# TensorE's small products of a chunked recurrence are queued group by group

## The chip, the cores and the metric

The kernel runs on one core of one Trainium2 chip. Times are device microseconds (us) of one execution. The core has five engines with a queue each, worked off in order: TensorE (PE, its weight loads PEld), VectorE (DVE), ScalarE (ACT), GpSimd (POOL) and SyncE (SP, which issues most DMAs). An instruction that waits for another engine holds up all that stands behind it in its queue.

## The reference

Three stages on [4 batches, 768 steps, 320 channels]. The first is a recurrence over the steps with a 40x40 state for each of 32 batch-heads; the second a feed-forward layer with a convolution of three steps and a gate; the third an attention with four experts of which two count.

```python
for t in range(S):                                   # state: [B, H, 40, 40]
    y[:, :, t] = einsum('bhd,bhde->bhe', r_t, state)
    Sa = einsum('bhde,bhe->bhd', state, a_t)
    state = state * w_t - einsum('bhd,bhe->bhde', Sa, b_t) + einsum('bhd,bhe->bhde', v_t, k_t)
x = relu-feed-forward(y): h = max(y @ w_in, 0); out = h * sigmoid(conv3(h)) @ w_out
out = attention of 4 experts on x, the best 2 of each row weighted by their gate
```

## The kernel before, in words

The recurrence is cut into chunks of 32 steps (24 chunks, `k`), two of which make a block of 64 (12 blocks, `n`). Three generators write its work. `prep(n)` forms for a block what doesn't depend on the state: decays on VectorE, the pairwise products of the inputs, and the inverse of a triangular matrix for each head. `chain(k)` carries the state over a chunk; each link needs the one before. `post(k)` forms the chunk's outputs. All three use TensorE for small products: 16 or 32 in a group (`mm`, L161), each on its own tiles of the PE array, or 4 transposes (`tr`, L165). In the trace and in the instruction order a group is known by what its products read:

- prep: `kb,a` (pairwise products, 32 products, two groups a block), `cst,kb` (transposes, four groups a block), `O,g` and `M,d` (inverse, 32 each, one group a block);
- chain: `SV,a` (32), `cst,sT` (transposes of the state, two groups), `X,T` (32), `VZ,KB` (16); ScalarE copies each result out before the next group can start (X at L360, VZ at L376, the new state SV in two instructions at L409), VectorE forms the new state (sT, L402 and L404);
- post: `cst,U` (transposes), `ra,VT` (16), `RB,LB` (32), with VectorE's mask RB (L441) and result xe (L455).

That makes 286 groups. A product in full float32 leaves two matmul records in the trace, a transpose one.

The feed-forward layer (`ff`, 128x128 matmuls at L561 and L584) runs beside the recurrence, and attention (L694 to L830) follows; the last part of the feed-forward layer runs beside the start of attention. `merge` calls the generators by due times: every `yield` tells when the next piece is due, `self.work` adds up what the small products are thought to cost, and the feed-forward layer advances by that sum.

What is called first has the higher priority. The order on every engine is then made by the tile framework when the program is built: it plays the program through on a timeline of its own, and gives each engine at each moment the ready instruction with the highest priority. So products of one group can be parted by products of another that became ready meanwhile and rank higher. [...]

Of the kernel before, what the change touches and what calls it, by code (L numbers as in the profile page):

```python
# [49 lines left out]
class Kernel:  # L50
# [103 lines left out]
    def load_rb(self, k):  # L154
        for h in range(2):
            self.nc.sync.dma_start(self.RB[R[1 - h], h].rearrange("p u a t -> p (u a t)"), self.i["rb"][k, 40 * h:40 * h + 40])

    def mm(self, ns, *a, **k):

        self.work += ns  # L160
        self.nc.tensor.matmul(*a, **k)  # L161

    def tr(self, ns, *a):
        self.work += ns
        self.nc.tensor.transpose(*a)  # L165

    def prep(self, n):
        nc, wk = self.nc, self.wk
        w, P, a, kb = self.w, self.P[n % 3], self.a[n % 2], self.kb
# [9 lines left out]
        for k in range(1, 5):  # L179
            x = early("xd", [128, 32, 16], "L1") if k == 1 else wk.tile([128, 32, 32 >> k], F32, name=f"L{k}", bufs=1)  # L180
# [34 lines left out]
        for u0 in (0, 8):  # L215
            us = slice(u0, u0 + 8)
            FG = self.ps[2][:, 0 if 0 < n < EN or n == 0 and u0 == 0 else 1].rearrange("p (u x s) -> p u x s", u=8, x=2)
            for u in range(8):
                for q in range(4):
                    be, r = q // 2, R[q % 2]  # L220
                    self.mm(WF, FG[32 * q:32 * q + 32, u].rearrange("p x s -> p (x s)"), a[r, be, q % 2, u0 + u],
                            kb[r, u0 + u, be].rearrange("p x s -> p (x s)"), start=True, stop=True)
                if u % 2:
                    yield 0.26 + 0.07 * (u0 > 0) + 0.015 * (u + 1) / 2
            nc.scalar.activation(Gp[:, us], FG[:, :, 1], AF.Copy)
            nc.vector.transpose(F[:, us], FG[:, :, 0])
            nc.gpsimd.tensor_tensor(F[:, us], F[:, us], self.mask[:, None].to_broadcast([128, 8, 32]), op=ALU.mult)
            yield 0.33 + 0.07 * (u0 > 0)
# [31 lines left out]
        def turn(u0):  # L260

            kp = self.ps[2][:, 1].rearrange("p (u x) -> p u x", u=4)
            for u in range(4):
                self.tr(WK, kp[:, u, :104], kb[E, u0 + u].rearrange("p b x t -> p (b x t)"), self.ident[:104, :104])
            nc.scalar.activation(KB[:, u0:u0 + 4], kp.rearrange("p u (h e) -> p u h e", h=2)[:, :, :, :40], AF.Copy)  # L265
# [16 lines left out]
        x = (8, 8)  # L282
# [25 lines left out]
        yield 0.72  # L308

        def blocks(out, lhs, rhs, x):  # L310
            for u in range(8):
                for q in range(0, 128, 32):
                    s = slice(q, q + 32)
                    self.mm(WS, out[s, u], lhs[s, u], rhs(s, u), start=True, stop=True)
                if u % 2:
                    yield x + 0.02 * (u + 1) / 2


        Mp = self.ps[2][:, 1, :256].rearrange("p (u x) -> p u x", u=8)
# [11 lines left out]
    def chain(self, k):  # L331
        nc, wk, t = self.nc, self.wk, self.t[k // NC]
        U, KB, u0 = self.U[k % 2], t["KB"], NP * (k % NC)
        zero = k == 0
        sT, sN = self.sT[k % 2], self.sT[(k + 1) % 2]

        def st(x):
            y = x[E]
            return bass.AP(tensor=y.tensor, offset=y.offset, ap=[list(y.ap[0]), [104, NP], [64, 2], [1, 40]])

        So, SV = self.S[k % 2], self.SV

        def back(p0):
            Sp = self.ps[3][:, 0].rearrange("p (m x) -> p m x", m=4)
            for p in range(4):
                self.tr(WR, Sp[E, p, :104], sT[E, p0 + p], self.ident[:104, :104])
            nc.scalar.activation(So[E, p0:p0 + 4], Sp[E].rearrange("p m (a e) -> p m a e", a=2)[:, :, :, :40], AF.Copy)

        cu = self.ps[0]
        Xp = cu[:, 0, :320].rearrange("p (m d) -> p m d", m=NP)  # L350
        for p in range(NP):
            for al in range(2):
                for be in range(2):
                    q = 32 * (2 * be + al)
                    r = slice(0, 96 + 8 * al)
                    self.mm(XA, Xp[q:q + 32, p], t["a"][r, be, al, u0 + p], SV[r, al, be, p], start=True, stop=True)
            if p == 3:
                yield 0.06
        X = wk.tile([128, NP, 40], F32, name="X", bufs=1)
        nc.scalar.activation(X, Xp, AF.Copy)  # L360
        yield 0.14
        if not zero:
            back(0)
            yield 0.25
        for p in range(NP):
            for al in range(2):
                for be in range(2):
                    q = 32 * (2 * be + al)
                    s, o = slice(q, q + 32), 64 * be + 32
                    self.mm(WX, cu[o:o + 32, al, p * 40:p * 40 + 40], t["T"][s, u0 + p], X[s, p], start=True, stop=True)  # L370
        VZ = self.VZ
        for be in range(2):
            s = slice(64 * be + 32, 64 * be + 64)
            y = VZ[s, :, :, be].rearrange("p m a d -> p a m d")
            z = cu[s, :, :320].rearrange("p a (m d) -> p a m d", m=NP)
            nc.scalar.activation(y, z, AF.Copy, scale=-1.0)  # L376
        yield 0.4
        if not zero:
            back(4)
            yield 0.5  # L380
        for p in range(NP):
            for al in range(2):
                self.mm(WD, cu[R[al], p // 4, 80 * (p % 4):80 * (p % 4) + 80], KB[:, u0 + p, al],
                        VZ[:, p, al].rearrange("p b d -> p (b d)"), start=True, stop=True)
        for be in range(2):
            s = slice(64 * be + 32, 64 * be + 64)
            for r in range(2):
                y, z = U[64 * r + 32 * be:64 * r + 32 * be + 32], VZ[s, r::2, :, be]
                y = bass.AP(tensor=y.tensor, offset=y.offset, ap=[list(y.ap[0]), [104, NP // 2], [64, 2], [1, 40]])
                if UD:  # L390
                    for al in range(2):
                        nc.sync.dma_start(U[64 * r + 32 * be:64 * r + 32 * be + 32, :, 64 * al:64 * al + 40], VZ[s, r::2, al, be])
                else:
                    nc.scalar.activation(y, z, AF.Copy)
        qq = t["q0"][E, u0:u0 + NP, :, None].to_broadcast([104, NP, 2, 40])
        for h in range(2):
            ps = slice(4 * h, 4 * h + 4)
            Dv = cu[E, h, :320].rearrange("p (m b d) -> p m b d", m=4, b=2)
            if zero:
                nc.vector.tensor_tensor(st(sN)[:, ps], Dv, qq[:, ps], op=ALU.mult)  # L400
            else:
                nc.vector.tensor_tensor(st(sN)[:, ps], Dv, st(sT)[:, ps], op=ALU.add)  # L402
        if not zero:
            nc.vector.tensor_tensor(st(sN), st(sN), qq, op=ALU.mult)  # L404
        if k + 1 < NT * NC:
            for al in range(2):
                y = sN[R[al]]
                y = bass.AP(tensor=y.tensor, offset=y.offset, ap=[list(y.ap[0]), [64, 2], [104, NP], [1, 40]])
                nc.gpsimd.tensor_copy(SV[R[al], al], y) if al < SC else nc.scalar.activation(SV[R[al], al], y, AF.Copy)  # L409
        if k + 1 < NT * NC:  # L410
            self.load_v(k + 1)
        yield 1.0

    def post(self, k):
# [10 lines left out]
        if c == 0:  # L425
            t["xe"] = wk.tile([128, NP, 2, TOK], F32, name="xe", bufs=1)
        vp = (self.ps[1] if k < BK else self.ps[3])[:, 0].rearrange("p (u x) -> p u x", u=4)
        for p in range(4):
            self.tr(WV, vp[E, p], self.U[k % 2][:, p], self.ident)
        nc.scalar.activation(VT[E].rearrange("p u b x -> p (u b) x")[:, :, 32:], vp[E].rearrange("p u (b t) -> p (u b) t", t=32), AF.Copy)  # L430
        yield 0.16
        ap = self.ps[3][:, 1].rearrange("p (u a t) -> p u a t", u=NP, a=2)
        for p in range(NP):
            for be in range(2):
                self.mm(WA, ap[64 * be:64 * be + 64, p], VT[E, p, be], ra[E, p, be], start=True, stop=True)
            if p == 3:
                yield 0.3
        for be in range(2):
            s = slice(64 * be, 64 * be + 64)
            y = RB[s, be].rearrange("p u a t -> p (u a) t")  # L440
# [2 lines left out]
        if k + 1 < NT * NC:  # L443
            self.load_ra(k + 1)
            self.load_vt(k + 1)
        yp = (self.ps[1] if k < BK else self.ps[3])[:, 1].rearrange("p (m b t) -> p m b t", m=NP, b=2)
        for p in range(NP):
            for be in range(2):
                r = slice(0, 104 + 24 * be)
                for al in range(2):  # L450
                    self.mm(WY, yp[R[al], p, be], LB[r, be, p, al], RB[r, be, p, al], start=True, stop=True)
            if p % 4 == 3:
                yield 0.55 + 0.05 * p
        pp = P.rearrange("p (c m b) t -> p c m b t", c=NC, b=2)[E, c]
        nc.vector.tensor_tensor(t["xe"][E, :, :, 32 * c:32 * c + 32], yp[E], pp, op=ALU.mult)  # L455
        yield 0.92
# [566 lines left out]
```

## Time and profile before

| | us |
|---|---|
| median of 3 runs | 898.44 (894.2 to 899.88) |
| the profiled execution's own time | 899.17 |
| its span, first to last instruction | 897.4 |
| recurrence with the feed-forward layer | about 45 to 590 of the span |
| attention alone | from about 650 on |

The profile is one execution, so sums are made against 899.17. Busy times of PE are modelled: matmuls overlap, so the time that a group takes is read from one start to the next, not from its length.

### The profile page before, as it was taken

The numbers are of one execution on the slowest core, as the hardware profiler recorded it, in microseconds if no ns is written. First come the engines' busy times: TensorE is split into PE (matmuls) and PEld (weight loads), VectorE is DVE, ScalarE is ACT, GpSimd is POOL, SyncE is SP. The second block draws the span as 40 slices with busy tenths as digits, with TensorE's granted clock in tenths as the row PEclk, the third lists the DMA queues.
The fourth block names the chain that finished last, engine by engine and source line by source line (L and its number), as shares of the span: only waits on it lengthen the run. The fifth ranks groups of instructions, "written<-read, shape, count | busy, mean of one in ns | idle before, by whom it ended". The sixth has DMA issues, their size and how long they took to land.

```text
span 897.4 us, 31509 instructions
## 1 busy us (share of the span) xinstructions
PE 748.3 (83%) x13112; PEld 657.7 (73%) x13112; DVE 693.9 (77%) x1541; ACT 574.4 (64%) x1355; POOL 377.6 (42%) x419
## 2 busy tenths in 40 slices
PE   1257768997988989888798879869999999999988
PEld 1146556785877977777687868859878888888876
DVE  5888896999898898787887984575677767876664
ACT  0156655866675767584758567758877666775565
POOL 6063545433335243322334242754644343443352
PEclk9999577997989799897979889979999999999999
DMA  5435673555564464545545534440011101110001
GB/s 129 94 122 125 166 167 86 134 127 127 116 158 104 99 152 108 132 99 130 129 113 120 117 86 93 90 127 16 15 46 37 46 16 31 37 38 16 23 8 38
DMA packets 143489, 81.17 MB, mean 90 GB/s; under 512 B 113859, under 2 KB 127043, under 8 KB 142387
## 3 DMA queue, kind: packets, MB, share of 16 engines
q1 hardware_dynamic: 138450, 74.34, 34.1%
q0 software_dynamic: 4896, 4.83, 2.5%
q8 instruction: 103, 1.69, 0.8%
q14 instruction: 40, 0.32, 0.1%
HBM read 51.63 MB, written 11.80 MB: 71 GB/s over the span
## 4 chain that ended last, share of the span: by engine, by line
PE 42%; DVE 24%; ACT 11%; DMA 10%; issue 7%; POOL 4%; SPq 1%; ACTq 0%; DVEq 0%; POOLq 0%
PE ps L161 8%; PE ps L561 5%; PE ps L584 5%; PE ps L815 4%; DVE cv L596 4%; PE ps L712 4%; PE ps L798 4%; PE ps L165 3%; PE ps L703 2%; PE ps L762 2%; PE ps L830 2%; DMA kb<-in_kb_e_dram 2%; DVE kb L205 2%; PE ps L763 2%; DVE Q L198 2%
## 5 line engine op out<-in xcount | busy, mean ns | idle before, releaser
L784 POOL TENSOR_TENSOR A<-A,rs 128x128 f32<-128x128 f32 (+5 forms) x96 | 87.7, 935 | 113.7 <-DVE rs L782 95.6
L596 DVE SCALAR_TENSOR_TENSOR cv<-h,cw,cv 128x256 f32<-128x256 f32 (+1 forms) x192 | 97.1, 550 | 38.5 <-ACT cv L594 37.7
L599 POOL TENSOR_TENSOR cv<-cv,h 128x512 f32<-128x512 f32 (+1 forms) x48 | 61.4, 1280 | 133.2 <-ACT cv L598 123.6
L561 PE MATMUL ps<-xl,win 128*128 128x256 f32 x384 | 97.1, 304 | 4.5 <-POOL xl L539 3.6
L561 PE MATMUL ps<-xh,win 128*128 128x256 f32 x384 | 96.5, 309 | 4.9 <-ACT xh L537 4.3
L584 PE MATMUL ps<-wout,gh 128*128 128x320 f32 x384 | 90.4, 330 | 2.6 <-ACT gh L478 2.5
L479 POOL TENSOR_TENSOR gl<-cv,gh 128x512 fp32r<-128x512 f32 x48 | 62.5, 1303 | 53.5 <-ACT gh L478 46.9
L769 ACT ACTIVATE A<-ps,nm 128x128 f32<-128x128 f32 (+5 forms) x96 | 60.7, 633 | 37.0 <-DVE nm L767 28.9
L561 PEld LDWEIGHTS ps<-xh,win 128*128 128x128 f32 x384 | 73.2, 210 | 7.0 <-ACT xh L537 4.6
L561 PEld LDWEIGHTS ps<-xl,win 128*128 128x128 f32 x384 | 73.1, 208 | 6.0 <-POOL xl L539 4.1
L767 DVE TENSOR_REDUCE nm<-ps 128x1 f32<-128x128 f32 (+5 forms) x96 | 58.8, 619 | 20.5 <-PE ps L765 8.9
L584 PEld LDWEIGHTS ps<-wout,gh 128*128 128x128 f32 x384 | 66.0, 200 | 4.9 <-ACT gh L478 4.1
L161 PE MATMUL ps<-kb,a 40*32 40x64 f32 x1536 | 34.3, 239 | 34.7 <-DVE kb L205 31.1
L584 PE MATMUL ps<-wout,gl 128*128 128x320 f32 x192 | 59.0, 330 | 0.3 <-issue 0.3
L165 PE MATMUL ps<-cst,kb 104*128 104x104 f32 x192 | 33.3, 307 | 29.4 <-ACT KB L265 16.4
L161 PE MATMUL ps<-RB,LB 104*40 104x32 f32 (+1 forms) x1536 | 47.9, 215 | 11.1 <-DMA RB<-in_rb_dram 5.0
L161 PEld LDWEIGHTS ps<-kb,a 40*32 40x32 f32 x1536 | 28.1, 120 | 39.0 <-issue 19.1
L161 PEld LDWEIGHTS ps<-RB,LB 104*40 104x40 f32 (+1 forms) x1536 | 41.6, 131 | 17.3 <-DVE cv L596 4.6
L798 PE MATMUL ps<-cid,A 128*128 128x128 f32 x336 | 52.9, 276 | 1.5 <-ACT AT L803 0.7
L762 PE MATMUL ps<-k,q 128*128 128x256 f32 (+3 forms) x144 | 49.3, 351 | 5.3 <-ACT A L769 3.8
L712 PE MATMUL ps<-x,wqk 128*128 128x384 f32 x256 | 53.2, 347 | 0.3 <-ACT yt L622 0.3
L598 ACT ACTIVATE cv<-cv 128x512 f32<-128x512 f32 (+1 forms) x48 | 30.3, 630 | 30.7 <-DVE cv L596 30.4
(177 smaller groups left out, 2191.6 us busy)
## 6 DMA issues: line engine op xcount, KB each, us to landing
kb<-in_kb_e_dram SPq DMA_DIRECT2D x24, 320.0 KB
LB<-KB SPq DMA_DIRECT2D x48, 160.0 KB
LB<-S SPq DMA_DIRECT2D x46, 100.0 KB
a<-in_a_e_dram SPq DMA_DIRECT2D x24, 160.0 KB
VT<-in_vt_dram SPq DMA_DIRECT2D x48, 80.0 KB
RB<-in_rb_dram SPq DMA_DIRECT2D x48, 80.0 KB
SV<-in_v_dram SPq DMA_DIRECT2D x48, 80.0 KB
VZ<-in_v_dram SPq DMA_DIRECT2D x96, 40.0 KB
```

The lines of the kernel that those rows point to most:

```text
L161: self.nc.tensor.matmul(*a, **k)
L165: self.nc.tensor.transpose(*a)
L479: (eng or self.nc.vector).tensor_tensor(lo, x, hi.bitcast(F32), op=ALU.subtract)
L561: nc.tensor.matmul(hp[:, dd], wt[:, 128 * d:128 * d + 128], x, start=k == 0, stop=k == 7)
L584: nc.tensor.matmul(self.ps[1][:, tb, :DM], x, wt, start=d == 0 and k == 0, stop=d == 7 and k == 2)
L596: nc.vector.scalar_tensor_tensor(y, h[:, dd, :, k:k + nt], self.cw[:, k, d:d + 1], y, op0=ALU.mult, op1=ALU.add)
L599: (nc.gpsimd if GM and st % GM == 0 and st >= GN else nc.vector).tensor_tensor(cv[:, :, :, :nt], cv[:, :, :, :nt], h[:, :, :, 1:1 + nt], o ...
L712: nc.tensor.matmul(pp, self.wqk[:, wk, hl, 128 * m:128 * m + 128], x[:, xk], start=j == 0, stop=j == 7)
L762: nc.tensor.matmul(sp[:, c0:c1], q[:, ce, 128 * j:128 * j + 128], k[:, ce, c0:c1], start=True, stop=False)
L769: nc.scalar.activation(A[:, :nk], sp[:, :nk], AF.Exp, bias=nm, accum_out=sums[:, e:e + 1])
L784: nc.gpsimd.tensor_tensor(A[:, :nk], A[:, :nk], rs[:, e:e + 1].to_broadcast([128, nk]), op=ALU.mult)
L798: nc.tensor.transpose(tp[:, m, e], As[e][:, 128 * (2 * g + m):128 * (2 * g + m) + 128], self.cid)
```

## The change

A group begins with `burst()`, which clears `head`. The group's first product is then issued at its own priority and kept as `head`. Every later one goes through `follow`: it is put behind `head` in PE's queue (`issue_after`), and ranks 3000 places higher, ahead of all that is ready. The due times inside a group are dropped: `yield` stands once, after the group. No product is added, removed or altered, and no tile or buffer either. Lines up to 157 keep their numbers; after it they move by 10 to 14, L161 and L165 become L172 (heads) and L175 (the rest).

```diff
+    def burst(self):
+
+        self.head = None
+
     def mm(self, ns, *a, **k):
+        self.follow(ns, self.nc.tensor.matmul, *a, **k)
+
+    def tr(self, ns, *a):
+        self.follow(ns, self.nc.tensor.transpose, *a)
+
+    def follow(self, ns, f, *a, **k):
 
         self.work += ns
-        self.nc.tensor.matmul(*a, **k)
-
-    def tr(self, ns, *a):
-        self.work += ns
-        self.nc.tensor.transpose(*a)
+        if self.head is None:
+            self.head = f(*a, **k).ins
+            return
+        with self.tc.issue_after(self.head), self.tc.high_priority(offset=3000):
+            f(*a, **k)
...
+            self.burst()
             for u in range(8):
                 for q in range(4):
                     be, r = q // 2, R[q % 2]
                     self.mm(WF, FG[32 * q:32 * q + 32, u].rearrange("p x s -> p (x s)"), a[r, be, q % 2, u0 + u],
                             kb[r, u0 + u, be].rearrange("p x s -> p (x s)"), start=True, stop=True)
-                if u % 2:
-                    yield 0.26 + 0.07 * (u0 > 0) + 0.015 * (u + 1) / 2
+            yield 0.26 + 0.07 * (u0 > 0) + 0.06
...
+        self.burst()
         for p in range(NP):
             for be in range(2):
                 r = slice(0, 104 + 24 * be)
                 for al in range(2):
                     self.mm(WY, yp[R[al], p, be], LB[r, be, p, al], RB[r, be, p, al], start=True, stop=True)
-            if p % 4 == 3:
-                yield 0.55 + 0.05 * p
+        yield 0.8
```

The other groups get `self.burst()` in the same way. More due times go or move: in `blocks` four become one, in `chain` that of SV,a moves to the group's end, in `post` that inside ra,VT is dropped.

Two places of PE's queue show it. A row is a line of the kernel, the operation, out<-in and the size, with a count where it repeats; a number behind a name is that of its buffer. The first place is in chunk 21: PE's queue before, with post's group RB,LB of chunk 20 in three pieces, the chain's SV,a and X,T of chunk 21 in two each, and prep's transposes (cst,kb) inside X,T.

```order
L161 MATMUL ps<-SV,a_81 32x40 x23
L161 MATMUL ps<-kb,a_82 32x64 x32
L161 MATMUL ps<-SV,a_81 32x40 x9
L165 MATMUL ps<-cst,sT_96 104x104 x4
L161 MATMUL ps<-RB,LB_85 40x32 x22
L161 MATMUL ps<-X,T 32x40 x10
L165 MATMUL ps<-cst,kb 128x104 x4
L161 MATMUL ps<-X,T 32x40 x22
L161 MATMUL ps<-RB,LB_85 40x32 x9
L165 MATMUL ps<-cst,kb 128x104 x4
L161 MATMUL ps<-RB,LB_85 40x32
```

The same RB,LB and X,T in PE's queue of the changed kernel, with what stands behind them.

```order
L172 MATMUL ps<-RB,LB_85 40x32
L175 MATMUL ps<-RB,LB_85 40x32 x31
L172 MATMUL ps<-cst,kb 128x104
L175 MATMUL ps<-cst,kb 128x104 x3
L172 MATMUL ps<-X,T 32x40
L175 MATMUL ps<-X,T 32x40 x31
L575 MATMUL ps<-xl,win 128x256 x2
L598 MATMUL ps<-wout,gh 128x320 x4
L172 MATMUL ps<-cst,kb 128x104
L175 MATMUL ps<-cst,kb 128x104 x3
```

Both groups stand whole; one set of prep's transposes is now ahead of X,T, the other behind it and behind feed-forward matmuls.

The second place is in chunk 11: PE's queue before, where the chain's VZ,KB cuts into post's RB,LB of chunk 10.

```order
L161 MATMUL ps<-RB,LB_85 40x32 x16
L161 MATMUL ps<-VZ,KB 40x80 x16
L161 MATMUL ps<-RB,LB_85 40x32 x15
L165 MATMUL ps<-cst,kb 128x104 x4
L161 MATMUL ps<-RB,LB_85 40x32
L165 MATMUL ps<-cst,U_92 104x128 x4
```

The same place in the changed kernel.

```order
L172 MATMUL ps<-RB,LB_85 40x32
L175 MATMUL ps<-RB,LB_85 40x32 x31
L172 MATMUL ps<-VZ,KB 40x80
L175 MATMUL ps<-VZ,KB 40x80 x15
L172 MATMUL ps<-cst,kb 128x104
L175 MATMUL ps<-cst,kb 128x104 x3
```

RB,LB is not cut any more, and the chain's VZ,KB stands behind all 32 of its products instead of behind 16.

## Rows read from the trace of the kernel before

**Rows 1.** The page: span, busy times, the chain by engine.

```profile
span 897.4 us, 31509 instructions
PE 748.3 (83%) x13112; PEld 657.7 (73%) x13112; DVE 693.9 (77%) x1541; ACT 574.4 (64%) x1355; POOL 377.6 (42%) x419
PE 42%; DVE 24%; ACT 11%; DMA 10%; issue 7%; POOL 4%; SPq 1%; ACTq 0%; DVEq 0%; POOLq 0%
```

**Rows 2.** Stretches: length, busy time of each engine, PE clock, DMA share, GB/s.

```profile
45.00:320.00 275.00, 221.38 (x5386) 193.15 (x5387) 237.73 (x459) 179.96 (x389) 118.90 (x122) 0.86 0.54 128
320.00:590.00 270.00, 228.93 (x5182) 206.77 (x5181) 214.18 (x404) 180.14 (x399) 106.90 (x108) 0.90 0.50 115
590.00:650.00 60.00, 53.95 (x370) 50.38 (x370) 38.75 (x91) 47.49 (x110) 32.31 (x36) 0.96 0.15 38
650.00:898.00 248.00, 234.89 (x1973) 199.95 (x1971) 170.66 (x509) 160.95 (x445) 103.30 (x124) 1.00 0.10 30
```

**Rows 3.** Chain by line, of 45 to 320 and of 320 to 590.

```profile
by line: PE ps L161 10.9%; issue 9.2%; PE ps L561 5.7%; DMA kb<-in_kb_e_dram 4.5%; DVE cv L596 4.5%; DVE kb L205 4.2%; PE ps L165 4.0%; PE ps L584 3.0%; DVE t L274 2.7%; ACT SV L409 2.6%; DMA xs<-xe 2.2%; DVE Q L198 2.1%; DMA xd<-xs 2.0%; A
...
by line: PE ps L161 15.6%; issue 10.3%; PE ps L584 7.8%; PE ps L561 7.5%; DVE cv L596 6.0%; DMA RB<-in_rb_dram 4.3%; PE ps L165 4.2%; DMA xs<-xe 3.1%; DMA LB<-S 2.3%; DVE Q L198 2.1%; DVE kb L205 2.1%; DMA SV<-in_v_dram 1.9%; DVE a L209 1.6
```

**Rows 4.** Stretches: PE and PEld busy with L161 alone, then with L165 alone.

```profile
45.00:320.00 275.00, 122.67 (x4736) 104.81 (x4736) 0.86 0.54 128
320.00:590.00 270.00, 100.40 (x4288) 86.62 (x4288) 0.90 0.50 115
...
45.00:320.00 275.00, 42.49 (x240) 28.36 (x240) 0.86 0.54 128
320.00:590.00 270.00, 32.89 (x216) 22.13 (x216) 0.90 0.50 115
```

**Rows 5.** Timeline of PE from 302.5: start, length, instruction, records; chunk 11's place.

```profile
302.55 0.81 PE L161 MATMUL ps<-RB,LB 104*40 104x32 f32 x32
303.18 1.29 PE L161 MATMUL ps<-VZ,KB 128*40 128x80 f32 x32
304.30 0.77 PE L161 MATMUL ps<-RB,LB 104*40 104x32 f32 x30
305.00 0.58 PE L165 MATMUL ps<-cst,kb 104*128 104x104 f32 x4
305.50 0.26 PE L161 MATMUL ps<-RB,LB 128*40 128x32 f32 x2
305.69 0.65 PE L165 MATMUL ps<-cst,U 128*104 128x128 f32 x4
```

**Rows 6.** Timeline of PE from 545.7: whole groups X,T, RB,LB and VZ,KB.

```profile
545.77 0.79 PE L161 MATMUL ps<-X,T 32*32 32x40 f32 x64
546.49 1.42 PE L161 MATMUL ps<-RB,LB 104*40 104x32 f32 x64
547.83 0.56 PE L584 MATMUL ps<-wout,gh 128*128 128x320 f32 x2
...
550.99 1.31 PE L161 MATMUL ps<-VZ,KB 128*40 128x80 f32 x32
552.22 0.53 PE L165 MATMUL ps<-cst,U 128*104 128x128 f32 x3
```

**Rows 7.** Timeline of PE from 518.9: chunk 21's place, [idle before <-releaser].

```profile
518.90 1.03 PE L161 MATMUL ps<-RB,LB 104*40 104x32 f32 x44
520.00 0.40 PE L161 MATMUL ps<-X,T 32*32 32x40 f32 x20
522.12 0.57 PE L165 MATMUL ps<-cst,kb 104*128 104x104 f32 x4 [1.71 <-DVE F L226]
522.62 0.62 PE L161 MATMUL ps<-X,T 32*32 32x40 f32 x44
523.17 0.57 PE L161 MATMUL ps<-RB,LB 128*40 128x32 f32 x18
526.81 0.96 PE L165 MATMUL ps<-cst,kb 104*128 104x104 f32 x4 [3.07 <-ACT KB L265]
527.70 0.34 PE L161 MATMUL ps<-RB,LB 128*40 128x32 f32 x2
527.97 1.44 PE L584 MATMUL ps<-wout,gh 128*128 128x320 f32 x4
```

**Rows 8.** Chain in order of time: a run of L584, and an ACT table load.

```profile
608.86 2.93 PE ps L584 x20
...
622.69 1.28 ACT L769
```

More of the change, by code (lines that the diff above doesn't have):

```diff
@@ L310, in blocks @@
         def blocks(out, lhs, rhs, x):
+            self.burst()
             for u in range(8):
@@ L314, in blocks @@
                     self.mm(WS, out[s, u], lhs[s, u], rhs(s, u), start=True, stop=True)
-                if u % 2:
-                    yield x + 0.02 * (u + 1) / 2
+            yield x + 0.08
         Mp = self.ps[2][:, 1, :256].rearrange("p (u x) -> p u x", u=8)
@@ L344, in back @@
             Sp = self.ps[3][:, 0].rearrange("p (m x) -> p m x", m=4)
+            self.burst()
             for p in range(4):
@@ L350, in chain @@
         Xp = cu[:, 0, :320].rearrange("p (m d) -> p m d", m=NP)
+        self.burst()
         for p in range(NP):
@@ L356, in chain @@
                     self.mm(XA, Xp[q:q + 32, p], t["a"][r, be, al, u0 + p], SV[r, al, be, p], start=True, stop=True)
-            if p == 3:
-                yield 0.06
+        yield 0.06
         X = wk.tile([128, NP, 40], F32, name="X", bufs=1)
@@ L364, in chain @@
             yield 0.25
+        self.burst()
         for p in range(NP):
@@ L380, in chain @@
             yield 0.5
+        self.burst()
         for p in range(NP):
@@ L427, in post @@
         vp = (self.ps[1] if k < BK else self.ps[3])[:, 0].rearrange("p (u x) -> p u x", u=4)
+        self.burst()
         for p in range(4):
@@ L432, in post @@
         ap = self.ps[3][:, 1].rearrange("p (u a t) -> p u a t", u=NP, a=2)
+        self.burst()
         for p in range(NP):
@@ L435, in post @@
                 self.mm(WA, ap[64 * be:64 * be + 64, p], VT[E, p, be], ra[E, p, be], start=True, stop=True)
-            if p == 3:
-                yield 0.3
         for be in range(2):
@@ L446, in post @@
         yp = (self.ps[1] if k < BK else self.ps[3])[:, 1].rearrange("p (m b t) -> p m b t", m=NP, b=2)
+        self.burst()
         for p in range(NP):
```

## The prediction, made before the changed kernel ran

> **What bounds the kernel now.** I read the page first, then the busy times by stretch, then the chain of waits of the recurrence, and last the timeline of PE at places where groups are cut. The page shows a program with no idle engine to speak of: PE is busy for 83% of the span, VectorE for 77%, and the chain that ended last runs through PE for 42% and through VectorE for 24% [rows 1]. The stretches part this in two. From 650 on PE is busy for 234.89 of 248 us: PE sets the end there, and the change touches none of its products. From 45 to 590, where the small products lie, PE is busy for 221.38 + 228.93 = 450.3 of 545 us and VectorE for 451.9 [rows 2]. Neither alone is the bound; work goes to and fro between PE, ScalarE and VectorE, and each queue waits in turn. The chain by line says how much of that is the small products: L161 and L165 have 10.9 + 4.0% of 275 us and 15.6 + 4.2% of 270 us [rows 3], that is 41.0 + 53.5 = 94.5 us. Their busy time in the same stretches is 122.67 + 100.40 + 42.49 + 32.89 = 298.4 us [rows 4]. So about a third (0.32) of what a small product costs lies on the path that sets the end; the other two thirds run while something else is late.
>
> **The change, part by part.**
>
> *Fewer turns from one group to another.* Counted in PE's order up to the last small product: 77 of the 286 groups are cut before, 16 after (14 of these are SV,a, whose second half waits for ScalarE's second copy of the state). Pieces of small groups fall from 401 to 300. What does a turn cost? Whole, RB,LB takes 547.83 - 546.49 = 1.34 us to the next start [rows 6]. In pieces it takes 0.63 + 0.70 + 0.19 = 1.52 us, VZ,KB and the transposes left out; its last product, 2 records, alone takes 0.19 us, where 1.34 / 64 x 2 would be 0.04 [rows 5]. So the odd piece costs about 0.15 us more. Not every turn costs that: VZ,KB takes 1.23 us when a transpose follows [rows 6], but 1.12 us when RB,LB does [rows 5], and these two use the same shape of the array (up to 128 rows by up to 64 columns), as the transposes do not. I therefore count only turns between unlike shapes: 390 before, 286 after, 104 fewer. Turns between like shapes stay at 98 and 97. At 0.15 us that is 15.6 us of PE time.
>
> [...] By a count of all turns, like or unlike, it would be 102 fewer at a lower mean price, some 13 us; the sum below hardly moves.
>
> How much of the 15.6 us reaches the end? By the chain's share 0.32, 5.0 us. If PE were the bound throughout, all 15.6. PE is busy for 83% of the recurrence [rows 2], which is nearer to the upper end, but VectorE is as busy, which speaks for the lower. I take 10 us, and keep 5.0 and 15.6 as bounds.
>
> *Cut groups that wait in the middle.* At 520.00 the chain's X,T gets 20 of its 64 records through; then prep's transposes stand in front and wait 1.71 us for VectorE, and X,T ends its issue at 523.17, 3.17 us after its start [rows 7], against 0.72 us whole [rows 6]. RB,LB of the same place is held open from 518.90 to 527.97 by two such waits, 1.71 and 3.07 us [rows 7]. Of the chain's groups the order has 8 X,T, 8 VZ,KB, 17 SV,a and 3 cst,sT cut before. Priced by the X,T row (2.4 us) the first two alone would be 16 x 2.4 = 38 us at most; the transposes and their waits don't vanish, they only stand elsewhere, so nothing is the other bound.
>
> *The chain can't cut in any more.* This goes the other way. Before, a link's group cuts 53 times into a group of prep or post that is under way; now it waits for the rest of it. At 303.18 VZ,KB cut into RB,LB with 32 records left, of which the next 30 took 0.70 us [rows 5]; in the changed order it stands behind all 64. By that row 53 x 0.7 = 37 us on the chain at most; nothing where the chain's group wasn't ready yet, or was held by the ScalarE copy ahead of it. The two terms are of one size and opposite sign, 38 against 37; I set their sum to 0, and keep a half of either, times the third that lies on the path (6 us), as its uncertainty in the likeliest case.
>
> *Feed-forward work is moved earlier.* Before the last small product the order now has 1060 feed-forward matmuls instead of 1028, since the whole group's cost is booked before the feed-forward layer is asked for more. 32 x 2.93 / 20 [rows 8] = 4.7 us leave the stretch in which PE is full and go into one with 95 us of idle PE. Bounds -4.7 and 0; I take -1, since PE there is busy when it isn't waiting.
>
> *ScalarE.* The order has 7 activation-table loads instead of 9: the last rounds of sigmoid and exponential, where the feed-forward layer ends beside attention, alternate less. One takes 1.28 us, and the one at 622.69 stands on the chain [rows 8]. Bounds -2.6 and 0; I take -1, PE being the busier engine there (53.95 of 60 us against 47.49 [rows 2]).
>
> *VectorE, POOL, DMA queues.* The same instructions in another order, up to a few places apart; no new wait is put in. Nothing of known sign; it widens the range.
>
> Sum: -10 + 0 - 1 - 1 = -12. Against the profiled execution's 899.17 that is 887.2; the median of the runs is 0.7 lower, so I say 887.0. A measurement of this kernel can tell about 1% from no change: 889.5 and below is faster, 907.4 and above slower.
>
> **Rivals.**
>
> *A. PE wasn't the limit.* Saved turns only make PE wait longer for VectorE and ScalarE. For it: VectorE is busy as long as PE from 45 to 590 [rows 2], and two thirds of the small products lie off the path [rows 3, 4]. Against it: the small products are still the largest item of that chain. It gives 899.2 - 5.0 - 1 = 893: within 1%.
>
> *B. The links wait for whole groups.* The 53 lost cuts hit the state's chain, of which every link waits for the one before, while the pieces now saved lay in groups that nobody waited for. For it: 32 of the 77 cut groups are RB,LB and ra,VT, whose results aren't needed by the next link. Against it: the chip runs a whole group in 0.72 to 1.34 us [rows 6], so a wait for the rest is short beside the link, which at 545 / 24 = 23 us has time for many of them. Its price is 37 us where each wait counts; at half of that, 18, less the 5.0 of rival A, it gives 899.2 + 13 = 912, slower. It decides from 37 x 0.35 = 13 us on, where it outweighs the 5.0 by the 8 us that count as slower.
>
> *C. The clock.* [...] Pieces of cut groups partly fill waits; whole groups leave the waits in one piece. If the mean falls from 0.88 to 0.85, PE's 450 us become 3.5% longer, 16 us, a third of it on the path: 5 us given back, 892, within 1%.
>
> [...]
>
> That the change doesn't do what it says is ruled out by the order, but for SV,a.
>
> **How the numbers follow.** The forecast (877 to 889) has 0.52, A 0.20, C 0.08, B 0.20. So faster 0.52, within 1% 0.28, slower 0.20. The range: down by all of the 15.6, the 4.7, the 2.6 and the 6 of uncertainty, some 29 us, to 870; up to about B's 912, rounded to 910, which leaves out somewhat over half of B. Within the likeliest case alone I would say 877 to 889.
>
> **What would show it.** Right: in the changed profile RB,LB and X,T stand as one row of 64 records at almost every chunk; the two stretches of the recurrence are shorter by about 10 us together; PE's busy time of L165 and L161 falls; attention's stretch keeps its length within 4 us. Wrong by A: the turns are gone, PE's waits for ACT and DVE rise by as much, the recurrence ends less than 6 us earlier. Wrong by B: the last small product comes later than before, and X,T and VZ,KB stand right behind RB,LB, ra,VT or kb,a on the chain. Wrong by C: the granted clock of 45 to 590 falls below 0.86.

## The result and the profile after

The changed kernel takes 899.96 us (median of 20 runs, 896.1 to 906.0), the kernel before 895.32 (20 runs beside them, 887.5 to 903.24): ratio 1.0059, 95% interval 1.004 to 1.0078. Forecast were 11 us less; measured are 4.6 us more, which is within 1% of no change. The two profiled executions can't show these 4.6 us by subtraction: they took 899.17 and 899.0 us, since before's lay 3.9 us above the median of its runs. What they show is what changed inside.

The page of the changed kernel, the lines that answer to [rows 1]:

```profile
span 897.2 us, 31501 instructions
PE 737.5 (82%) x13112; PEld 654.9 (73%) x13112; DVE 692.4 (77%) x1541; ACT 568.4 (63%) x1353; POOL 371.6 (41%) x419
PE 38%; DVE 24%; ACT 17%; issue 8%; DMA 7%; POOL 4%; SPq 1%; ACTq 0%; DVEq 0%; POOLq 0%
```

PE is busy for 10.8 us less, and the end did not come earlier. ScalarE's share of the chain rose from 11 to 17%, PE's fell from 42 to 38. The stretches, as in [rows 2]:

```profile
45.00:320.00 275.00, 209.20 (x5338) 187.74 (x5339) 230.67 (x452) 179.30 (x394) 118.91 (x125) 0.85 0.52 126
320.00:590.00 270.00, 230.97 (x5244) 210.28 (x5242) 221.27 (x416) 180.00 (x400) 103.51 (x108) 0.88 0.49 116
590.00:650.00 60.00, 54.15 (x363) 49.94 (x364) 38.43 (x84) 43.51 (x104) 31.11 (x35) 0.95 0.15 41
650.00:898.00 248.00, 234.20 (x1963) 199.56 (x1961) 168.51 (x509) 159.25 (x443) 101.05 (x122) 1.00 0.10 30
```

From 45 to 590 PE is busy for 440.2 us instead of 450.3, VectorE for 451.9 as before. In attention's stretch PE is busy for 234.2 us (234.9 before). The last small product starts at 576.5 us (574.3 before) by PE's timeline, the last feed-forward product at 651.2 (657.3). The chain by line in the two stretches of the recurrence answers to [rows 3]:

```profile
by line: PE ps L175 11.6%; issue 11.5%; DVE cv L610 5.0%; ACT U L408 4.4%; PE ps L575 4.0%; PE ps L172 3.4%; ACT VZ L389 3.1%; POOL wx L509 2.5%; DVE sT L418 2.4%; PE ps L598 2.3%; ACT T L311 2.2%; DVE kb L215 2.1%; POOL cv L613 2.1%; ACT S
...
by line: PE ps L175 15.0%; issue 10.1%; PE ps L598 6.1%; PE ps L575 5.8%; DVE cv L610 5.3%; PE ps L172 4.5%; DMA xs<-xe 4.4%; DVE kb L215 2.6%; DVE Q L208 2.3%; DVE a L219 2.2%; DVE L L194 2.2%; ACT cv L608 2.1%; ACT h L583 2.0%; ACT SV L42
```

The small products, now L172 and L175, have 15.0% of 275 and 19.5% of 270 us, 93.9 us in all. They had 94.5. [rows 4] have no counterpart: heads and rest overlap, and their busy times can't be added. With every overlap counted once, the small products are busy for 276.8 us from 45 to 590, and were for 288.8. PE's timeline at chunk 21 shows the groups whole, where [rows 7] had them in pieces:

```profile
523.67 0.22 PE L172 MATMUL ps<-RB,LB 104*40 104x32 f32 x1
523.68 0.22 PE L175 MATMUL ps<-RB,LB 104*40 104x32 f32 x1
523.73 0.20 PE L172 MATMUL ps<-RB,LB 104*40 104x32 f32 x1
523.74 1.35 PE L175 MATMUL ps<-RB,LB 104*40 104x32 f32 x61
525.02 0.31 PE L172 MATMUL ps<-cst,kb 104*128 104x104 f32 x1
...
526.32 0.77 PE L175 MATMUL ps<-X,T 32*32 32x40 f32 x59
```

RB,LB takes 525.02 - 523.67 = 1.35 us, as whole groups did before [rows 6]. So the change does what it says. What PE got for it is seen 100 us earlier in the same timeline:

```profile
415.81 0.28 PE L575 MATMUL ps<-xl,win 128*128 128x256 f32 x1
420.92 0.27 PE L172 MATMUL ps<-X,T 32*32 32x40 f32 x1 [4.83 <-DVE T L339]
```

PE stands for 4.83 us ahead of X,T. Over 24 chunks the first product of X,T waits 18.2 us in all, where it waited 3.5 before; all of PE's waits from 45 us to the last small product are 97.7 us instead of 87.4. What grew are its waits for VectorE, from 24.6 to 40.4 us; those for ScalarE stayed (40.6 and 41.2). T, the other factor of X,T, is formed by prep and ends on VectorE. PE's waits for it, first in the kernel before, then in the changed one (engine, tile and line, what it waited for, us in total, times, longest):

```profile
PE ps L161 <- DVE T L328: 0.4, 1, 0.4
PE ps L172 <- DVE T L339: 14.3, 5, 5.6
```

VectorE's own waits for ScalarE and PE from 45 to 590, of the changed kernel, the largest:

```profile
DVE cv L610 <- ACT cv L608: 32.1, 16, 7.7
DVE F L236 <- ACT G L235: 15.8, 10, 3.7
DVE d L317 <- ACT tmp L316: 7.2, 5, 2.8
DVE sT L416 <- PE ps L175: 5.7, 3, 3.8
DVE RB L455 <- PE ps L175: 4.3, 3, 2.1
DVE xe L469 <- PE ps L175: 3.8, 3, 2.4
DVE F L236 <- ACT hc L589: 2.5, 1, 2.5
```

The same of the kernel before:

```profile
DVE cv L596 <- ACT cv L594: 26.9, 14, 4.1
DVE F L226 <- ACT G L225: 12.2, 8, 3.0
DVE xe L455 <- PE ps L161: 9.2, 3, 4.6
DVE sT L402 <- PE ps L161: 7.0, 3, 2.6
DVE wvg L479 <- ACT wvg L478: 5.3, 1, 5.3
DVE RB L441 <- PE ps L161: 4.1, 4, 2.3
DVE d L306 <- ACT tmp L305: 3.1, 5, 1.2
```

Added up over the whole views, VectorE's waits for PE fell from 21.9 to 13.8 us and those for ScalarE rose from 48.2 to 58.2; all its waits together are 84.7 us and were 84.4. So VectorE waits for somebody else, but not longer. These are readings of one execution of each, leads and no proof.

### The profile page after: what moved, and what is told of

The parts are those of the page before. It is cut to its first block, busy times and chain, and to the rows that moved or that the text cites. A ratio compares the mean times of both kernels' runs of the same rounds, so it can differ in the third digit from the quotient of the medians.

```text
span 897.2 us, 31501 instructions
## 1 busy us (share of the span) xinstructions
PE 737.5 (82%) x13112; PEld 654.9 (73%) x13112; DVE 692.4 (77%) x1541; ACT 568.4 (63%) x1353; POOL 371.6 (41%) x419
## 3 DMA queue, kind: packets, MB, share of 16 engines
q0 software_dynamic: 4896, 4.83, 2.3%
## 4 chain that ended last, share of the span: by engine, by line
PE 38%; DVE 24%; ACT 17%; issue 8%; DMA 7%; POOL 4%; SPq 1%; ACTq 0%; DVEq 0%; POOLq 0%
PE ps L175 8%; DVE cv L610 4%; PE ps L726 4%; PE ps L829 4%; PE ps L812 3%; PE ps L598 3%; PE ps L575 3%; PE ps L172 3%; PE ps L717 2%; PE ps L776 2%; PE ps L844 2%; ACT U L408 2%; ACT A L783 2%; PE ps L777 2%; ACT h L583 1%
## 5 line engine op out<-in xcount | busy, mean ns | idle before, releaser
L610 DVE SCALAR_TENSOR_TENSOR cv<-h,cw,cv 128x256 f32<-128x256 f32 (+1 forms) x192 | 106.2, 590 | 40.3 <-ACT cv L608 39.9
L798 POOL TENSOR_TENSOR A<-A,rs 128x128 f32<-128x128 f32 (+5 forms) x96 | 87.7, 935 | 97.7 <-DVE rs L796 51.3
L598 PE MATMUL ps<-wout,gh 128*128 128x320 f32 x384 | 93.0, 339 | 6.6 <-ACT gh L492 5.1
L598 PEld LDWEIGHTS ps<-wout,gh 128*128 128x128 f32 x384 | 69.8, 211 | 7.9 <-ACT gh L492 6.0
L829 PE MATMUL ps<-AT,v 128*64 128x128 f32 x672 | 47.7, 280 | 2.6 <-ACT AT L817 2.5
L389 ACT ACTIVATE VZ<-ps 32x640 f32<-32x640 f32 x48 | 33.5, 697 | 23.0 <-PE ps L175 22.0
L726 PEld LDWEIGHTS ps<-x,wqk 128*128 128x128 f32 x256 | 43.2, 189 | 3.9 <-DVE q L734 1.7
L408 ACT ACTIVATE U<-VZ 32x320 f32<-32x320 f32 x96 | 44.9, 468 | 1.6
L812 PEld LDWEIGHTS ps<-cid,A 128*128 128x128 f32 x336 | 38.5, 140 | 8.5 <-issue 3.4
```

The lines of the kernel that those rows point to most:

```text
L598: nc.tensor.matmul(self.ps[1][:, tb, :DM], x, wt, start=d == 0 and k == 0, stop=d == 7 and k == 2)
L610: nc.vector.scalar_tensor_tensor(y, h[:, dd, :, k:k + nt], self.cw[:, k, d:d + 1], y, op0=ALU.mult, op1=ALU.add)
L726: nc.tensor.matmul(pp, self.wqk[:, wk, hl, 128 * m:128 * m + 128], x[:, xk], start=j == 0, stop=j == 7)
L798: nc.gpsimd.tensor_tensor(A[:, :nk], A[:, :nk], rs[:, e:e + 1].to_broadcast([128, nk]), op=ALU.mult)
L812: nc.tensor.transpose(tp[:, m, e], As[e][:, 128 * (2 * g + m):128 * (2 * g + m) + 128], self.cid)
L829: nc.tensor.matmul(op[64 * e:64 * e + 64], v[:, kt, 128 * pr + 64 * e:128 * pr + 64 * e + 64], ATs[kt][:, e], start=kt == n - 1, stop=kt = ...
```

## The experiments

Most kernels below are the kernel before with the queues of all engines held in before's order, and only PE's list edited. The hold is the same in each:

```diff
         Kernel(tc, ins, {"out": out}).run()
+        pin(tc, nc)
...
+        for a, b in zip(names, names[1:]):
+            tc.add_manual_dep(ins[b], a, mybir.DependencyInfo(mybir.DependencyClass.NoSync, mybir.DependencyReason.DATA), reason="pin")
```

Each edit is shown by a place or two of PE's list that it alters. "Clock" is the mean granted clock over the runs; before's lay between .924 and .928 in the five sets of runs.

**1. All 77 cut groups whole, where their last piece stood; turns 390 to 266.**

```diff
-L161 MATMUL ps<-kb,a_82 32x64 x31
 L161 MATMUL ps<-O_326,g_99 32x32 x32
-L161 MATMUL ps<-kb,a_82 32x64
+L161 MATMUL ps<-kb,a_82 32x64 x32
```

> The order of the kernel before is kept on every engine, and on PE too, but for the 77 cut groups: their earlier pieces move down to the last one, so each group ends where it ended in the queue and nobody stands behind it longer than before. Turns between unlike array shapes fall from 390 to 266. This is the saving alone. 'Turns cost time' (the prediction): 124 turns x 0.15 us = 18.6 us of PE, 0.65 of which reaches the end: 10 to 14 us faster than before, and the loss seen with the change (4.6 us) comes from what else was moved. 'PE wasn't the limit': at most 0.32 x 18.6 = 6 us faster, and as likely nothing, since the pieces that ran early also filled waits of PE. 'Links wait for whole groups': faster by any amount, as no link waits longer here.

903.25 us against 895.72, ratio 1.0111 [1.0074, 1.0148], clock .9125. Its page:

```profile
span 903.0 us, 31492 instructions
PE 730.3 (81%) x13112; PEld 648.5 (72%) x13112; DVE 696.5 (77%) x1541; ACT 574.2 (64%) x1355; POOL 373.5 (41%) x419
```

PE is busy for 18.0 us less than before [rows 1], and the kernel is slower; the pieces also moved to other places. What one turn costs can't be had from such differences. By 18.0 / 124 it would be 0.145 us, by the change's 10.8 / 104 it would be 0.104. But two kernels of experiments 5 and 8 have only 23 and 29 turns fewer, and PE is busy for 12.7 and for 2.0 us less (links_whole_at_first, then others_of_post_at_last):

```profile
PE 735.6 (83%) x13112; PEld 647.8 (73%) x13112; DVE 694.4 (78%) x1541; ACT 573.0 (64%) x1355; POOL 378.8 (43%) x419
PE 746.3 (83%) x13112; PEld 655.8 (73%) x13112; DVE 691.6 (77%) x1541; ACT 574.4 (64%) x1355; POOL 380.8 (42%) x419
```

**2. Only the groups of prep and post that the chain cut (34), whole where their first piece stood.**

```diff
-L161 MATMUL ps<-ra,VT 64x64 x13
-L165 MATMUL ps<-cst,kb 128x104 x4
-L161 MATMUL ps<-ra,VT 64x64
+L161 MATMUL ps<-ra,VT 64x64 x16
+L165 MATMUL ps<-cst,kb 128x104 x4
 L161 MATMUL ps<-X,T 32x40 x32
-L161 MATMUL ps<-ra,VT 64x64 x2
```

> The order of the kernel before is kept on every engine but PE, where the 34 groups of prep and post that a group of the chain cuts into are made whole at their first piece: the chain's group now stands behind the rest. Turns fall from 390 to 322. 'Links wait for whole groups': 10 us or more slower than before, or at least as much slower than the kernel whose groups are whole at their last piece. 'PE wasn't the limit': within 3 us of before either way. 'Turns cost time': 68 x 0.15 x 0.65 = 6.6 us faster.

898.47, ratio 1.0047 [1.0012, 1.0083], clock .914. This is rival B's mechanism with the turns that it saves: 4.2 us (1.1 to 7.4), not 18.

**3. The rank alone**, with before's due times inside the groups; against the changed kernel, at SV,a:

```diff
+            if p == 3:
+                head = self.head
+                yield 0.06
+                self.head = head
```

> The change without its new due times: the products of a group follow their head at the higher rank, but every due time inside a group stands as before, so the program is traced in the same sequence as before. 285 turns, 13 groups cut. If the rank makes the change slower, this is 3 to 6 us slower than before, as the change is; if the due times do, it is at or below before (0 to 10 us faster).

904.82, ratio 1.0118 [1.0075, 1.0161].

**4. The due times alone**, without the rank; against the changed kernel:

```diff
-        if self.head is None:
-            self.head = f(*a, **k).ins
-            return
-        with self.tc.issue_after(self.head), self.tc.high_priority(offset=3000):
-            f(*a, **k)
+        f(*a, **k)
```

> The new due times alone, without the rank: 364 turns and 74 cut groups, so nearly as many as before; the last small product has 882 feed-forward matmuls ahead of it instead of 1028. If the due times cost the change its gain, this is 5 us or more slower than before. If only the rank matters, it is within 3 us of before. If any reshuffle of the order moves the time by some us, it may lie 5 us off on either side, with the share of chain and engines much as before.

924.36, ratio 1.0339 [1.0288, 1.039]. Only 882 feed-forward products stand before the last small one (1028 before); the rest run when the recurrence is over, and the last one starts at 683.6 us. The change's two halves each cost more than both together.

**5. The chain's groups apart from those of prep and post.** First the chain's 36 cut groups (17 SV,a, 8 X,T, 8 VZ,KB, 3 cst,sT) whole at the last piece:

```diff
-L161 MATMUL ps<-X,T 32x40 x22
-L165 MATMUL ps<-cst,kb 128x104 x4
-L161 MATMUL ps<-X,T 32x40 x10
+L165 MATMUL ps<-cst,kb 128x104 x4
+L161 MATMUL ps<-X,T 32x40 x32
```

> Order of the kernel before on every engine but PE; there only the chain's 36 cut groups (17 SV,a, 8 X,T, 8 VZ,KB, 3 cst,sT) are made whole, at their last piece; prep's and post's groups stay cut. Turns 390 to 334. New theory, 'early pieces were free': a group's first piece ran while its second half waited for another engine; put behind the wait, its 0.2 to 0.6 us come on top, at a group that the next link needs. Then this alone is 5 us or more slower than before and makes up most of the 9.9 us by which all groups at their last piece were slower. 'Turns cost time': 56 x 0.15 x 0.65 = 5 us faster.

895.99, ratio 0.999 [0.9953, 1.0028], clock .926. The other 41 (21 RB,LB, 11 ra,VT, 7 kb,a, O,g, cst,U) at the last piece:

```diff
-L161 MATMUL ps<-RB,LB_85 40x32 x25
 L161 MATMUL ps<-M_101,d_100 32x32 x32
 L161 MATMUL ps<-VZ,KB 40x80 x16
-L161 MATMUL ps<-RB,LB_85 40x32 x7
+L161 MATMUL ps<-RB,LB_85 40x32 x32
```

> As the run before, but only prep's and post's 41 cut groups (21 RB,LB, 11 ra,VT, 7 kb,a, 1 O,g, 1 cst,U) are made whole, at their last piece. Turns 390 to 316. 'Early pieces were free': prep's and post's groups have slack, so no more than 4 us slower, and the two halves add up to the 9.9 us. If all three kinds of group matter alike, this is 5 us slower. 'Turns cost time': 74 x 0.15 x 0.65 = 7 us faster.

899.29, ratio 1.0062 [1.0031, 1.0093], clock .914. The chain's X,T, VZ,KB and cst,sT whole at the first piece, so that the state comes sooner:

```diff
-L161 MATMUL ps<-X,T 32x40 x25
+L161 MATMUL ps<-X,T 32x40 x32
 L161 MATMUL ps<-O_1425,g_99 32x32 x32
-L161 MATMUL ps<-X,T 32x40 x7
```

> Order of the kernel before on every engine but PE; there the 19 cut groups X,T, VZ,KB and cst,sT of the chain are made whole at their first piece: the rest of the group goes ahead of what cut in (mostly prep's transposes that wait for VectorE or ScalarE). SV,a stays cut. Turns 390 to 367. If the state's chain sets the pace, these groups end up to 2.4 us earlier each, and the kernel is 4 to 12 us faster than before. If something else sets the pace (VectorE's work, prep's own chain through the transposes), it is within 3 us of before.

894.87, ratio 0.9984 [0.995, 1.0018], clock .922. Both of these last edits together:

```diff
-L161 MATMUL ps<-VZ,KB 40x80 x11
...
+L161 MATMUL ps<-VZ,KB 40x80 x16
+L165 MATMUL ps<-cst,kb 128x104 x8
+L161 MATMUL ps<-RB,LB_86 40x32 x32
```

> Both: the chain's 19 cut groups whole at their first piece, prep's and post's 41 whole at their last; SV,a stays cut. 295 turns, 16 groups cut, nearly as in the change (286 and 16), but the chain never waits for the rest of another group. 'Links wait for whole groups': this takes away all that the change cost and is 5 us or more faster than before. 'Early pieces were free': the sum of the two runs it is made of.

900.34, ratio 1.0058 [1.0031, 1.0084], clock .917. So it makes no measurable difference whether the chain's own groups are cut, come early or late. The hold of the queues can't cost much either, as both kernels have it. The loss, as large as that of the change, goes with the groups of prep and post.

**6. Post apart from prep**, of those 41, at the last piece. Post's 33:

```diff
-L161 MATMUL ps<-RB,LB_85 40x32 x4
 L161 MATMUL ps<-kb,a_81 32x64 x8
-L161 MATMUL ps<-RB,LB_85 40x32 x16
+L161 MATMUL ps<-RB,LB_85 40x32 x32
```

> Of the 41 groups only post's 33 (21 RB,LB, 11 ra,VT, 1 cst,U) whole at their last piece. 336 turns instead of 390. If post's groups carry the loss: 1.004 to 1.008. If the few groups of prep do (theory: prep's products come late and the vector engine waits): 0.998 to 1.002.

902.06 against 895.7, ratio 1.0052 [1.0015, 1.009], clock .919. Prep's 8:

```diff
-L161 MATMUL ps<-kb,a_81 32x64 x8
...
-L161 MATMUL ps<-kb,a_81 32x64 x24
+L161 MATMUL ps<-kb,a_81 32x64 x32
```

> Of the 41 groups only prep's 8 (7 kb,a, 1 O,g) whole at their last piece. 369 turns. If prep's groups carry the loss: 1.004 to 1.008; if post's do: 0.998 to 1.002. If both do in part, each lies between, and the two add up to about 0.6%.

896.96, ratio 1.0031 [1.0001, 1.0061], clock .920. Both lose some. Their intervals overlap, so which loses more isn't shown.

**7. Filling PE's waits**, to see whether the clock does it: extra products of the constant unit matrix ahead of products that waited.

```diff
+        for _ in range(n):
+            if wide:
+                self.nc.tensor.transpose(self.ps[0][:, 1, 320:448], self.ident, self.ident)
+            else:
+                op(a[0], *[self.like(x) for x in a[1:]], **k)
+        op(*a, **k)
```

> The kernel before with every engine's order kept, and 655 extra TensorE products (transposes or small products of the constant unit matrix, their results overwritten or never read) put ahead of 39 products for which TensorE waited 0.5 us or longer between 45 and 580 us in the profiled run, sized to fill about three quarters of each wait. If the granted clock follows from TensorE's own waiting (theory: the clock), the mean clock of the runs rises from .925 by .01 or more and the time falls, by 2 to 3 us per .01 as the spread of single runs suggests: 0.990 to 0.997 of before. If the clock has no part in it (theory: waits alone), the clock may rise but the time doesn't fall: 1.000 to 1.005, since filled waits sometimes overrun.

918.87, ratio 1.024 [1.0194, 1.0287], clock .941. The same on the order with prep's and post's 41 groups whole:

> The kernel whose 41 groups of prep and post are whole at their last piece (1.0062 without filling, mean clock .914), with 624 extra products put in the same way into 47 waits of its own profiled run. Theory the clock: the clock comes back to .925 or above and with it the time, 0.995 to 1.000. Theory waits alone: the time stays at 1.005 or above, whatever the clock.

913.02, ratio 1.0184 [1.0141, 1.0227], clock .942. PE's timeline of the first kernel at one filled place, and the wait there in the kernel before:

```profile
458.94 4.36 PE L178 MATMUL ps<-cst 104*40 104x32 f32 x109
463.10 0.22 PE L180 MATMUL ps<-RB,LB 104*40 104x32 f32 x1
```

```profile
447.46 0.62 PE L161 MATMUL ps<-RB,LB 104*40 104x32 f32 x10 [4.43 <-DMA RB<-in_rb_dram]
```

There the filling is about as long as the wait was (4.16 us from its start to that of RB,LB, against 4.43). Elsewhere it overran: the 94 products at the first place took 20.15 us for a wait of 7.57. So this pair raised the clock but was no clean test of it. With less in it, the same edit on before's order, and the first place left out:

> The filling again with less: 205 extra products at 32 waits after 50 us, about 28 us of work by their slower rows for 60 us of waits. Theory the clock sets the time: the mean clock rises by .005 or more above .925 and the ratio is 0.994 to 0.999. Theory waits and TensorE's queue set it: 1.000 to 1.008, as what is put in still delays the products behind it.

902.53 against 892.96, ratio 1.0101 [1.0065, 1.0137], clock .930. A higher clock, and slower again. But at 25 of the 32 places the trace has no wait left behind the filling, so here too it may have held up the products behind it. That the clock is without effect isn't shown by these three.

**8. Lost cover.** In before, pieces of post's groups stood between SV,a and X,T, where PE waits for X or T. Only the 11 groups that do so whole at the last piece:

```diff
-L161 MATMUL ps<-ra,VT 64x64 x13
-L165 MATMUL ps<-cst,kb 128x104 x4
-L161 MATMUL ps<-ra,VT 64x64
+L165 MATMUL ps<-cst,kb 128x104 x4
 L161 MATMUL ps<-X,T 32x40 x32
-L161 MATMUL ps<-ra,VT 64x64 x2
+L161 MATMUL ps<-ra,VT 64x64 x16
```

> Before's order, and of post's 33 cut groups only the 11 of which pieces stand between the last SV,a and the first X,T of a chunk whole at their last piece (365 turns). Theory lost cover: these 11 carry the loss, ratio 1.003 to 1.007, and the waits ahead of X,T grow from some 4 us to 10 us or more. Theory it is something else (the clock, any regrouping of post): no more than its share of 33 groups, 1.000 to 1.002.

897.63, ratio 1.0059 [1.003, 1.0088], clock .923; X,T waits 11.3 us. Just as the theory has it, but the other 22 groups, of which no piece stood between SV,a and X,T, do the same:

```diff
-L161 MATMUL ps<-RB,LB_85 40x32 x12
 L161 MATMUL ps<-M_101,d_100 32x32 x32
-L161 MATMUL ps<-RB,LB_85 40x32 x4
...
+L161 MATMUL ps<-RB,LB_85 40x32 x32
```

> The other 22 of post's 33 cut groups whole at their last piece (361 turns). Theory lost cover: 0.997 to 1.001, and X,T's waits stay near 4 us. Theory something else: 1.003 to 1.005.

897.85, ratio 1.0059 [1.0028, 1.0089], clock .925. X,T waits 7.7 us, less than in the kernel just above but more than the 3.5 of before, so this isn't the clean opposite that was expected. And with cover given back from the feed-forward layer:

```diff
+L584 MATMUL ps<-wout,gh 128x320 x4
+L561 MATMUL ps<-xh,win 128x256
+L561 MATMUL ps<-xl,win 128x256
 L161 MATMUL ps<-X,T 32x40 x32
 L161 MATMUL ps<-RB,LB_86 40x32 x32
-L584 MATMUL ps<-wout,gh 128x320 x4
-L561 MATMUL ps<-xh,win 128x256
-L561 MATMUL ps<-xl,win 128x256
```

> The kernel with prep's and post's 41 groups whole at their last piece (1.0062), and at ten places where X,T waited in its profiled run the next 6 to 16 feed-forward products (108 in all, 13.5 us of waits) put ahead of X,T. Theory lost cover: the waits ahead of X,T fall from 15.7 us to under 8 us and the ratio to 1.000 or less. Theory it is the clock or anything else: 1.004 or more although X,T waits less.

908.84, ratio 1.0173 [1.0127, 1.022], clock .9125. X,T waits only 2.2 us, and the kernel is slower by a further 1%. But the products put ahead overran. Counted from the later of X's and T's end, X,T starts late by 40.1 us in all over the 24 chunks, against 20.3 in the kernel that this one is built on (others_whole_at_last) and 28.2 in before. So this run doesn't settle it. What stands against lost cover as the whole cause is the run before it: the same loss with less of X,T's waiting.

**9. The price of a microsecond.** First less work for TensorE, every queue in before's order:

```diff
                     for k, (wt, x) in enumerate(ops):
-                        nc.tensor.matmul(hp[:, dd], wt[:, 128 * d:128 * d + 128], x, start=k == 0, stop=k == 7)
+                        if st >= 38 or k not in (2, 5):
+                            nc.tensor.matmul(hp[:, dd], wt[:, 128 * d:128 * d + 128], x, start=k == 0, stop=k == 7)
```

> Before's order without 152 of the feed-forward layer's first products (two products of the weights' low part with xh, of eight per sum, in the first 38 steps, left out: the low part of those weights is missing from the result). [...]

897.52 against 897.85, ratio 1.0012 [0.9987, 1.0037], clock .914. The recurrence's stretches:

```profile
45.00:320.00 275.00, 216.76 (x5414) 188.54 (x5416) 240.07 (x465) 182.91 (x396) 119.20 (x125) 0.86 0.52 128
320.00:590.00 270.00, 219.17 (x5001) 195.80 (x5002) 211.98 (x398) 176.87 (x393) 104.67 (x106) 0.88 0.49 114
```

PE is busy for 435.9 us, 14.4 less than before [rows 2]. At the chain's share of 0.32 these 14.4 us would have brought 4.6, with PE as the limit throughout all of them; the interval leaves at most 1.2 us of gain. The clock fell too, from .924 to .914, so what the missing work may have brought and what the clock may have cost can't be told apart here. Then less for VectorE:

```diff
-                    for k in (1, 2):
+                    for k in (1, 2) if st >= 38 or dd == 0 else (1,):
```

> Before's order without 38 of the 152 scalar_tensor_tensor instructions of the feed-forward layer's convolution (one tap for one of two halves in the first 38 steps left out), 38 x 0.527 us = 20 us of VectorE. Theory VectorE sets the recurrence's pace: 10 to 20 us less, 0.978 to 0.989. Theory neither engine alone does and both are worth their share of the chain (0.24 to 0.30): 5 to 6 us less, 0.993 to 0.995. If its time isn't the limit: 0.998 to 1.002.

888.07, ratio 0.991 [0.9874, 0.9946]. The group in the kernel before (45 to 590; count | busy, mean ns | idle before):

```profile
L596 DVE SCALAR_TENSOR_TENSOR cv<-h,cw,cv 128x256 f32<-128x256 f32 x152 | 73.4, 527 | 27.4 <-ACT cv L594 26.9
```

By this mean 38 x 0.527 = 20.0 us of VectorE work are left out; by the page it is busy for 16.2 us less (693.9 before [rows 1]):

```profile
PE 743.7 (84%) x13112; PEld 654.8 (74%) x13112; DVE 677.7 (77%) x1503; ACT 573.1 (65%) x1355; POOL 374.8 (42%) x419
```

They bring 8.1 us (4.8 to 11.3), 0.4 to 0.5 us for each. The clock was .931 against .924, which may be part of it. It is the only kernel of all that beats the one before, and it leaves work out.

## Why the prediction was wrong

**The step that failed** is "How much of the 15.6 us reaches the end? ... I take 10 us, and keep 5.0 and 15.6 as bounds." What the runs show in its place is no gain at all: 152 products fewer, 14.4 us of PE's time, brought 1.2 us at most, at a clock lower by .01 (experiment 9), and neither did the 18.0 us by which PE is less busy in experiment 1 make that kernel faster. The lower bound, 0.32 of the saving, came from the chain's share. A share of the chain says how often PE was the last to arrive. It doesn't say that the end moves when PE is sooner there; another engine can then be last a moment later. The change's profile fits that: PE is busy for 10.1 us less from 45 to 590, and up to the last small product it waits 10.3 us more, above all for VectorE. Zero had to be a bound. The share is not always wrong, though. L596 on VectorE held 28.6 us of the chain [rows 3] for 73.4 us of busy time, 0.39, which is near the price measured for it; L561 on PE held 35.9 us for 103.3, 0.35, and a microsecond of it brought nothing. The shares are alike; only the runs tell the two engines apart.

That 899.96 lies between 870 and 910 is luck: the upper end stood there for rival B, whose mechanism cost far less than its price.

**The saving itself**, 15.6 us, is neither confirmed nor refuted. PE's busy time fell by 10.8 us, but between single profiles it moves by as much with few turns saved (experiment 1). That only a turn between unlike shapes costs anything rests on two rows, 1.12 against 1.23 us [rows 5, 6]; no run tried it. Two slips of the working change nothing in the argument: by its own counts all turns are 105 fewer (390 + 98 against 286 + 97), not 102, and 887.2 less 0.7 is 886.5.

**Cut groups and lost cuts**, set to 0 as two terms of some 38 us each, with 6 us kept for error: each was far smaller, but the sum isn't 0. The chain's groups can be whole or not, early or late, for nothing measurable (0.999, 0.9984). The lost cuts cost 4.2 us (experiment 2), and the same kind of groups cost as much when they are put late, where they hold up no link (1.0062). That is a cost of whole groups of prep and post for which the prediction had no term. The trace of before has one reading that fits the chain's indifference: at 7 of the 12 block starts T was ready after X, by 51.2 us in all, so that the link waited there for prep and not for its own products. No run tried it.

**The terms of -1 each** (feed-forward work, ScalarE's tables): the last feed-forward product starts 6.1 us sooner and ScalarE loads 7 tables instead of 9; no run priced either.

**Rival A** had the mechanism that the runs bear out best: the turns are gone, PE waits 10.3 us more. Its own 5.0 us of gain were wrong for the same reason as mine. VectorE's time does have a price there, 0.4 to 0.5 us for one.

**Rival B** was the side on which the time fell, with a mechanism worth about a quarter of its 18 us. And the loss doesn't need a link that waits: it is as large with the groups put late.

**Rival C**: the clock of the recurrence did fall, 0.86 and 0.90 to 0.85 and 0.88, the mean over the runs to .917. The sign named for it, below 0.86 from 45 to 590, was just missed (0.865). Before, it was below 1.00 in the 60 us after the recurrence too, 0.96 [rows 2]. That waits left in one piece lower the clock was the author's guess, and no run shows that they do. The clock can't be the whole loss, since two kernels lose the same 0.6% at nearly before's clock (.923, .925). It isn't ruled out as a part. Over 121 runs of the kernel before, in five sets, a clock higher by .01 went with a time shorter by 1.5 us (give or take 0.7). By that, as an estimate, the change's clock stands for some 1 to 2 of the 4.6 us, if the clock is a cause there and not a consequence. The kernel with .914 that loses nothing has less work, and the slower ones with .930 to .942 have more, so they decide nothing.

Occupancy couldn't decide here: PE and VectorE were busy alike, 450.3 and 451.9 of 545 us [rows 2], and a price was measured for VectorE's time alone.

**What stays open** is the 4.6 us themselves. They go with whole groups of prep and post; that much the runs show. Which wait carries them they don't. Halves of post's groups cost 0.6% each and together 0.5%; the runs that filled waits held up other products, or may have. That PE now waits for prep's T (14.3 us against 0.4) was read from one execution of each and not tried. A part for the clock isn't ruled out.

## What to carry to other kernels

Before a saving on an engine is counted, price a microsecond of it: hold every queue in its order, leave some 20 us of that engine's work out, and see whether the end moves. Look at the clock beside it: with 152 products left out here it fell from .924 to .914. Let zero be a bound wherever two engines are busy alike, whatever share of the chain the one has. And where in-order queues feed each other, work that is cut up can stand in waits; gathering it here took 10 us off PE's busy time and put as much into its waits.

## What was not expected of the hardware

TensorE's granted clock went with its own work in both directions: 152 products fewer took the mean over the runs from .924 to .914, and 205, 624 and 655 more brought .930, .942 and .941 against .925 and .9275. The same products with all groups whole took it to .9125 (experiment 1), so their places count as well as their number. In the changed kernel PE waits 10.3 us more up to the last small product, and the mean clock is .917 (before's lay between .924 and .928); no run shows whether the waits lower it.
